# Whole or tiled turns on TensorE in an attention-then-mixing kernel, with a new order of its steps

## The chip, the cores and the metric

The kernel runs on one core of one Trainium2 chip. The metric is the device time of one execution in microseconds; the median of three timed runs of the kernel before is 230.54 us. Engines are named as in the profile: PE (TensorE, matmuls), PEld (its weight loads), DVE (VectorE), ACT (ScalarE), POOL (GpSimd) and SP (SyncE, which only issues DMAs here; a few of the last stores are issued by ACT).

## The reference: what is computed

For 8 batches, 8 heads, 576 positions and 64 features per head, attention is computed twice: once on q, k and v averaged over groups of four positions (144 of them) and repeated fourfold, and once locally, each position looking at those less than four away. The two are added and taken as x, 576 x 512 per batch. Then x is mixed:

```python
theta = x @ w_theta
zr, zi = x * np.cos(theta), x * np.sin(theta)
y = np.einsum('ts,bsd->btd', w_tok_r, zr) + np.einsum('ts,bsd->btd', w_tok_i, zi)
u = x + y
return (u + np.maximum(u @ w_ch, 0.0)).astype(np.float32)
```

Inputs and the output are float32; inside, the kernel works in bfloat16 with float32 sums.

## The kernel before, in words

The work of all eight batches is cut into named steps, and one string, `ORDER`, lists them: some 1190 words. A word's first two letters name the kind of step, the rest its place: the banks of PSUM on which a PE step works (`tp67`: banks 6 and 7), the engine of a copy (`a` ACT, `v` DVE, `g` POOL) or the staging slot of a load (base 36). Each kind is handed its batches and parts in ascending order, so the string alone fixes the order. After each word the function `pin` ties every instruction to the one before it on its engine; each engine, and SP's queue of DMAs, thus runs exactly in the order of the string, each at its own pace, and semaphores hold it where data or buffers are not ready. Three batches or so are under way at a time.

Per batch the steps are:

- `lk`, `lq`, `lv`, `lw`: loads of k, q (four of 288 KB each) and v into 16 staging slots, issued on SP. `ck`, `cq`, `cv`: their casts to bfloat16. Line 295 casts q and k, line 396 v.
- `tp` (function `tp`, line 302): turns a pair of head pairs of k or q, [positions, features], to [features, positions]. A partition holds nine positions, so that nine blocks are turned into two PSUM banks. `ev` (line 315) copies the result out to `kT` and `qT`. For batch 7 the DMA turns them (`dk`).
- `kd`, `qd`: sums over four positions (lines 321, 329 to 335). `pv`, `vd`: the same for v.
- `sd`, `ed`, `nd`, `xn`, `xd`, `xc`: the averaged attention, up to its turned result `xdT`.
- `ps` (line 482), `ex`, `mk`: local scores, exponential and band, in blocks of 64 positions; `po` (line 515) and `nm` (lines 523 and 524): times v, and the division, into `tmp`.
- `xt` (line 537): turns the local result by matmuls against an identity, in units of two, two and one chunks per batch (a chunk is 116 positions). `xa` (line 545) adds the averaged result and writes `xT`.
- `th`, `cs`, `tt`, `ct`: theta and its cosine and sine (line 556 on PE, 561 and 562 on ACT). `xm`, `zz`, `zt`, `zp`, `zc`: x turned and multiplied by them, into `z`. Batches 6 and 7 turn x by DMA (`dx`).
- `mx` (line 636) and `ua` (line 641): the mix over tokens, eight groups of nine matmuls, and the addition of x.
- `up`, `uc` or the DMA `du`: u turned back. `ch` (line 666), `rl` (line 674) and `st`: the channel product, the rectified sum and the store; `ht`, `rt`, `ss`, `sr` do this for the last 64 positions, two batches at a time.

Once, at the start, the weights are loaded and cast (`la`, `ca`, `lb`, `cb`, `lc`, `cc`), the token weights are turned on PE (`wp`, `wc`), and v of batch 0 goes its own way (`l1`, `c1`, `t1`, `e1`, `x1`). `wm` words (line 764) are matmuls on zeros: the bank, a number of 512-column ones and one of so many times 64 columns. `te` and `ts` touch the exponential or the sine on ACT.

Each PE step uses the array in one of these shapes: whole (128x128) for `tp`, `xm`, `up`, `th`, `tt`, `mx`, `ch`, `ht`, `wp`, `nd` and `xd`; 64x64 tiles for `ps`, `po`, `sd` and `xt`; 128 rows by 32 or 64 columns for `pv` and `x1`. In a row of the profile the shape stands ahead of the operands, as in `64*64 64x58`.

Of the kernel before, what the change touches and what calls it, by code (L numbers as in the profile page):

```python
# [63 lines left out]
wcv xm2 cbg xm0 zz zp7 tp45 cs qdg wp3 wp6 zz wcv lw zz wcv wcv zca eva wp7 wcv wp1 wca te wp0 wcv ps34 ps56 ex ex
ps12 mx0 lq1 cvg lk2 lka mx7 lqc mx3 qdv cvg ua lk7 ex ua lk0 mkv mkv kdg sd67 po45 nm sd12 lq4 cva lk5 lk9 cvg cvg ed
ed mx0 ua ua lq3 pv67 po45 po23 nm mx0 vda mkg nd67 lk8 nd45 lkb nm xn xn lq6 ckg ckg tp12 mx3 po45 ua lca ua nm cqg
cqg tp67 eva eva xd0 ckg ckg up1 lq7 po23 lvc xcv nm tp45 xt67 cqg mx0 cqg xt23 eva xt45 lv4 qdg kdg uca lw lv0 lw lw
lv3 lv1 lw lw xa xa tp67 cka ts ckg ckg th1 th2 xa th5 lk8 xm4 evv cs cqg xm1 ckv th3 zz tt4 up6 lq6 lqb cs zz tp12
xm7 ua cs ucv ct cs cqg eva te ztv xm6 zz zz mx0 ua tp34 zp7 tp56 ps12 zcv mx7 mx0 ex cvv kdg evv eva lk7 lk9 cvg lk4
qdg ua up7 uca sd12 mkv ps34 po56 ex ua ccv lcc lc5 kdg nm mkv mx0 sd34 ed po56 cvg cvg ua cqg mx7 nm ua ed mx0 ua lk2  # L70
cka cqg ps67 lqd lq0 cva po45 nm lca ex po23 ckg ckg nm pv01 lvb mx6 vda lk6 utv lw tp45 eva lv1 lw cca ccv nd01 nd23
ua xn xn qdg tp67 mx5 eva lv8 lv9 cqg cqg lw lw ccg ps34 qdg ps67 ua ps12 kdv ex ex xd0 lva xca lw mkg mkg lqc lq0 ch5
rl ckg ckg cvg cvg ch3 sd67 xt45 mkg ed rl ex ts mx0 xa xt67 po45 lv5 th1 cs xa nm ua tp23 th7 up4 up1 ucv xt56 xa mkv
lv4 ch0 eva po56 po23 cvg lq2 tt4 uca th1 cs th7 nm st nm xm2 lqb rl lq1 zz lqd ct cvg xm6 lw cqg ch5 cs zz cs cqa te
up0 up1 rl sd23 ucv po67 ch4 nm rl ch0 rl ucv tp67 lv7 ed cvg pv45 vdv lk8 lk9 eva st st tp23 eva xm0 ztg lk0 lka lw
xm1 zz zz zp7 ch6 zca lvc lv3 kdg nd45 xn nd23 ckg tp01 cva xn qdg utg mx7 cka ps23 rl kdg eva ps01 ua po45 mx6 up7 ex
ex lw lw lv8 nm qdg lw cqg po45 cqg ucv lvb lv2 lw sd23 sd01 lv5 ed mx7 lw lw ua tp23 nm xd4 ed ckg ckg xca st evv
tp01 eva mx6 mkg xt45 xt23 ua ua cva cvg cvg xt01 cka ts cvg xa xa mx7 th6 xa po45 nm pv23 tt0 th1 lk4 xm4 st st mkg
th5 vdv st cs nd23 ua zz ct cqg cqg ztg tp67 th4 cs dt po01 cs cs te xn evv po23 mx5 kdg qdg xm4 xm6 mx7 nm ps01 ex nm
ps23 ua lvd ua ex ch5 ps01 ex qdg zz lw lw xm7 zz rl kdg zp6 zz mkg nd23 xn lv1 lva lv3 mx5 zca sd67 lw ps01 ex po34  # L80
mx2 ua lw ed tp01 sd67 cva nm po34 eva cvv cvg ed lw up5 uca ua mx2 cvg nm cvg lvc xd3 ua pv04 xcv lk7 lk0 mx7 lq9 lq6
lq2 lqd lq8 lqb lq5 ckg ckg vda lq7 lw xt56 mkv cqg cqg po34 lk4 xt01 xa xa ch2 st cva ts lv6 th5 up6 ckg xm0 nm th1
tp34 cs ucv cs mkg rl eva mx6 ua ua th1 xt67 lk0 lk1 cs cqa po45 mkv xa nm ht3 rt tp67 th1 eva zz xm2 lv9 xm3 xm4 lw
lve zz zz ckg dk4 kdv mx0 cqg tp67 nd23 xn cs zz ua cqa eva mx1 nd67 xn cqa sr cqa cka tt2 ct dkb up4 cva cva ua mx0
mx7 ua cvg cvv uca te po01 nm qdg kdg qdg sd56 ed po23 ua ch4 rl xd0 ch1 ztg lw nm up7 ch4 uca xca po23 dz xt67 rl evg
ckg nm st st pv15 vda mx0 ps23 xa ex rl up1 up7 evg ua ucv mx6 uca ss ps01 ex xt45 cqa utg xa ua lv1 dk4 ps23 ex mx7
up0 uca th4 lvb sd56 mkv po23 lw lw xt01 utg dt ua dk7 cvv nm th7 du ed ts evg nd56 xa nd23 tt0 xn xn ct qdg mkv mkg
evv mx1 ztg xd2 up0 ua cs ch3 rl cs te mx4 ch7 qdg ps56 rl xcv ua mx1 ex cvg po23 po45 ua uca ps67 ex ht1 nm nm st st
rt cva ss mx0 ua po67 xt45 nm ps23 st xa ex ts du kdg th1 xm0 xm7 cs th6 cs xm4 zz zz zz ch5 rl kdg mx7 ua th0 po67 nm
cs te xt45 xa sd12 ch3 xm0 ch7 ch4 xt56 st ed sd12 mkg mkg ed ts zz dz lw mx0 lv1 du du cvv lw cvg th1 cs rl uta mx3  # L90
st rl rl xa dxb ua po45 po67 pv02 nm nm ua du mx1 vda ch4 dx mkg ua po23 po01 po67 rl sr nm mx5 ua mx4 tt5 dx1 du nm
nm nd23 xn nd01 st mx6 th7 mx2 cs xn xd3 mx0 ua ua xcv ua ua xt67 utv ct dx st st xt45 xt23 xa ch1 rl th0 ch6 ch1 ch7
cs xa xa tt0 zz zz th2 th3 cs st du du ch4 rl zz zz ztg ct dz rl mx2 mx0 mx1 cs ua ua st dxe dx ht0 ua th1 cs th3 dx7
dx zz st st mx2 rl mx1 ua ua cs zz dt mx3 mx1 mx2 zz zz ztg dz mx7 ua mx3 du du du mx6 rt ua ua utg ua st rl du st mx7
mx4 ua ua ua sr mx7 mx6 mx5 ua ua ua du du ua ch7 ch6 ss ch5 rl rl ch7 ch6 ch4 ch3 du du st uta dt sta rl st rl ht7
ch2 sta rl st rl sta rl st rt ssa sr rl sta rm su k0
"""


# [1 line left out]
def kernel(  # L101
# [161 lines left out]
    at = {}  # L263
# [32 lines left out]
        return step  # L296

    def tp(b, i, n, w):
        ps = at["tp", b, i, n] = pair(w).rearrange("p k e -> p (k e)").bitcast(BF16)
        t = tm[n][(2 * b + i) % TM]  # L300
        for r in range(WR):
            nc.tensor.transpose(out=ps[:, P * r:P * r + P], in_=t[:, r, :, :], identity=ident)  # L302
# [15 lines left out]
    def means(src, dst, w):
        with nc.allow_low_precision(reason="sums are taken in float32 and rounded once"):
# [205 lines left out]
                                in0=ps[:, :, :, 0:D], in1=r.unsqueeze(3).to_broadcast([P, 2, 4, D]), op=ALU.mult)  # L525

    def xt(b, u, w):
        ps = at["xt", b, u] = pair(w).rearrange("p k (x n) -> p (k x) n", x=2)
        for i, c in enumerate(UNITS[u]):
            t = tmp[(NCH * b + c) % NTMP]  # L530
            for g in range(2):
                n = 2 * c + g
                lo = STEP * n - W0[n]
                for j in range(4):
                    for hf in range(2):
                        r = slice(W * hf, W * hf + W)
                        nc.tensor.matmul(out=ps[W * (j % 2):W * (j % 2) + W, 2 * hf + j // 2,  # L537
                                                CH * i + STEP * g:CH * i + STEP * g + OWN[n]],
                                         lhsT=t[r, g, D * j:D * j + D], rhs=ident[r, W * hf + lo:W * hf + lo + OWN[n]],
                                         start=True, stop=True)  # L540
# [267 lines left out]
```

## Time and profile before

| | |
|---|---|
| timed runs | 230.54, 230.37, 230.74 us |
| span of the profiled execution | 232.2 us |
| share of the span in which the engine is busy | PE 94%, DVE 81%, ACT 67%, POOL 62% |
| costliest lines on PE | L636 (`mx`) 78.0 us, L556 (`th`) 30.8, L666 (`ch`) 29.8 |
| lines of the change on PE | L302 (`tp`) 252 matmuls, 19.2 us; L537 (`xt`) 640 matmuls, about 10 us |
| moved by DMA | 49.41 MB, 213 GB/s in the mean |

The profile gives the profiled execution's span, from the first instruction to the last; no other time was kept of that execution. A row of a group reads: line, engine, operation, output and inputs, shape, count, then busy time and the mean duration of one, then the idle time ahead of it and what ended it. The busy time of PE counts an instruction until its result has gone through the array, so neighbours overlap: the time that a group takes from PE is read from the start of its first instruction to the start of the next group's first.

### The profile page before, as it was taken

The page shows a single profiled execution, that of the slowest core. Times are in us where ns is not written, and L with a number is a line of the kernel's source. Part 1 is how long each engine was busy: PE and PEld are TensorE (multiplying, and loading weights), DVE is VectorE, ACT ScalarE, POOL GpSimd, SP SyncE. Part 2 cuts the span into 40 slices and gives each one's busy share as a digit, 9 for nine tenths or more (in the row PEclk, how much of TensorE's full clock was granted, in tenths as well). Part 3 has the DMA queues.
Part 4 walks back from the last instruction along what each step waited for, and adds up shares of the span by engine and source line. Part 5 has one row for each costly group of instructions (what it writes and reads, how often), then busy time and mean ns, then how long its engine had stood idle before and what let it go on. Part 6 is the DMA issues. An engine that isn't in the chain of part 4 may idle for free.

```text
span 232.2 us, 9404 instructions
## 1 busy us (share of the span) xinstructions
PE 217.7 (94%) x3943; PEld 152.6 (66%) x3970; DVE 187.7 (81%) x367; ACT 156.2 (67%) x243; POOL 145.0 (62%) x192
## 2 busy tenths in 40 slices
PE   7997899999999999899999989989998999999992
PEld 3655678877877666776775675756655775668741
DVE  5699888999988799789968887698986978558473
ACT  4589799689988898898877978778788232430000
POOL 7689977879985999879963489598952001100000
PEclk9999799999999999999999999999999999999999
DMA  6999968997999689968999996892284358656587
GB/s 217 395 390 390 291 114 238 361 300 118 265 391 179 165 245 285 243 142 214 205 165 347 307 213 115 206 153 92 67 149 109 71 127 193 138 159 137 142 227 245
DMA packets 76795, 49.41 MB, mean 213 GB/s; under 512 B 61136, under 2 KB 61392, under 8 KB 76752
## 3 DMA queue, kind: packets, MB, share of 16 engines
q1 hardware_dynamic: 76096, 47.76, 81.9%
q10 hardware_dynamic: 656, 1.05, 1.3%
q8 instruction: 31, 0.51, 0.9%
q14 instruction: 12, 0.10, 0.1%
HBM read 33.98 MB, written 9.44 MB: 187 GB/s over the span
## 4 chain that ended last, share of the span: by engine, by line
PE 60%; DMA 10%; POOL 10%; issue 6%; ACT 5%; DVE 4%; SPq 4%; DVEq 0%; POOLq 0%; ACTq 0%
PE PS L636 21%; PE PS L666 9%; PE PS L556 8%; DMA st<-in_q_dram 6%; PE PS L302 4%; POOL two L329 3%; PE PS L515 2%; SPq L347 2%; DMA st<-in_k_dram 2%; PE PS L537 2%; DMA ur<-uT 2%; POOL q_tm L295 2%; PE PS L482 2%; PE PS L447 1%; PE PS L595 1%
## 5 line engine op out<-in xcount | busy, mean ns | idle before, releaser
L636 PE MATMUL PS<-WT,z 128*128 128x288 bf16 x576 | 78.0, 287 | 0.0
L636 PEld LDWEIGHTS <-z 128*128 128x128 bf16 x576 | 53.9, 98 | 15.9 <-issue 1.3
L641 DVE TENSOR_TENSOR uT<-PS,xT 128x288 bf16<-128x288 f32 x64 | 28.6, 452 | 12.7 <-PE PS L636 10.9
L561 ACT ACTIVATE cs<-PS,pihc 128x512 bf16<-128x512 f32 x32 | 22.0, 689 | 21.1 <-PE PS L556 13.4
L556 PE MATMUL PS<-wth,xT 128*128 128x512 bf16 x116 | 30.8, 383 | 0.7 <-issue 0.2
L666 PE MATMUL PS<-wch,uT 128*128 128x512 bf16 (+1 forms) x122 | 29.8, 373 | 0.9 <-issue 0.6
L524 DVE TENSOR_TENSOR tmp<-PS,rl 128x512 bf16<-128x512 f32 x40 | 27.7, 692 | 1.4
L545 DVE TENSOR_TENSOR xT<-PS,xdT 128x928 bf16<-128x928 f32 (+1 forms) x24 | 22.3, 952 | 3.7 <-PE PS L537 2.3
L674 DVE SCALAR_TENSOR_TENSOR osb<-PS,ur 128x512 f32<-128x512 f32 x28 | 19.1, 687 | 7.1 <-DMA ur<-uT 3.0
L490 ACT ACTIVATE pm<-PS 128x1024 bf16<-128x1024 f32 (+1 forms) x24 | 20.5, 880 | 6.2 <-PE PS L482 6.1
L577 POOL TENSOR_TENSOR zT<-xT,cst 128x512 bf16<-128x512 bf16 x7 | 9.7, 1383 | 20.6 <-ACT cst L574 20.6
L295 POOL CAST k_tm<-st 128x576 bf16<-128x576 f32 x23 | 15.1, 668 | 11.2 <-DMA st<-in_k_dram 11.1
L396 POOL CAST v_w<-st 128x512 bf16<-128x512 f32 x21 | 13.3, 651 | 10.6 <-DMA st<-in_v_dram 10.5
L770 ACT ACT_TABLE_LOAD x15 | 19.2, 1283 | 0.3
L666 PEld LDWEIGHTS <-uT 128*128 128x128 bf16 x132 | 11.9, 98 | 11.2
L562 ACT ACTIVATE cs<-PS 128x512 bf16<-128x512 f32 x32 | 19.1, 597 | 0.0
L556 PEld LDWEIGHTS <-xT 128*128 128x128 bf16 x128 | 11.7, 99 | 10.6 <-issue 0.6
L295 POOL CAST q_tm<-st 128x576 bf16<-128x576 f32 x23 | 15.4, 686 | 4.9 <-DMA st<-in_q_dram 4.7
L503 POOL TENSOR_TENSOR pm<-pm,band 128x512 bf16<-128x512 bf16 x16 | 18.3, 1164 | 0.0
L329 POOL TENSOR_TENSOR two<-qT 128x576 f32<-128x576 bf16 x14 | 16.5, 1177 | 0.7 <-ACT qT L315 0.4
L620 DVE TENSOR_TENSOR z<-PS,cs 128x1024 bf16<-128x1024 bf16 x24 | 15.8, 684 | 0.5 <-ACT cs L562 0.3
L437 ACT ACTIVATE pd<-PS 128x864 bf16<-128x864 f32 x16 | 13.8, 889 | 2.5 <-PE PS L426 2.5
(124 smaller groups left out, 422.9 us busy)
## 6 DMA issues: line engine op xcount, KB each, us to landing
st<-in_k_dram SPq DMA_DIRECT2D x32, 288.0 KB, 6.5
st<-in_q_dram SPq DMA_DIRECT2D x32, 288.0 KB, 6.3
st<-in_v_dram SPq DMA_DIRECT2D x70, 128.0 KB, 5.2
out_dram<-osb SPq DMA_DIRECT2D x26, 256.0 KB, 4.0
st<-in_v_dram SPq DMA_DIRECT2D x4, 288.0 KB, 3.5
st<-in_moe_w_tok_r_dram SPq DMA_DIRECT2D x4, 288.0 KB, 6.5
st<-in_moe_w_tok_i_dram SPq DMA_DIRECT2D x4, 288.0 KB, 7.2
st<-in_moe_w_theta_dram SPq DMA_DIRECT2D x4, 256.0 KB, 6.7
```

Of the source, the lines that this page charges most:

```text
L295: COPY[w](out=to, in_=of)
L329: nc.gpsimd.tensor_tensor(out=t, in0=src[:, :, 0:2], in1=src[:, :, 2:4], op=ALU.add)
L490: nc.scalar.activation(out=pm[(3 * b + u) % NPM][:, :, 0:n].rearrange("p e c j w -> p e (c j w)"), in_=at.pop(("ps", b, u))[:, :, 0:4 * W ...
L524: nc.vector.tensor_tensor(out=tmp[(NCH * b + c) % NTMP].rearrange("p g (j d) -> p g j d", d=D), in0=ps[:, :, :, 0:D], in1=r.unsqueeze(3).t ...
L545: nc.vector.tensor_tensor(out=xT[b % 2][:, :, lo:lo + cnt].rearrange("p e (m j) -> p e m j", j=4), in0=at.pop(("xt", b, u))[:, :, 0:cnt].r ...
L556: nc.tensor.matmul(out=ps, lhsT=xT[b % 2][:, dc, P * c:P * c + P], rhs=wth[:, dc, :], start=(dc == 0), stop=(dc == 3))
L561: nc.scalar.activation(out=t[:, 0, :], in_=ps, func=AF.Sin, bias=pihc, scale=1.0)
L562: nc.scalar.activation(out=t[:, 1, :], in_=ps, func=AF.Sin, bias=0.0, scale=1.0)
L636: nc.tensor.matmul(out=ps, lhsT=z[b % 2][:, j, P * dc:P * dc + P], rhs=WT[:, j, cols], start=(j == 0), stop=(j == 8))
L641: nc.vector.tensor_tensor(out=uT[b % 2][:, dc, cols], in0=at.pop(("mx", b, i)), in1=xT[b % 2][:, dc, cols], op=ALU.add)
L666: nc.tensor.matmul(out=ps[:, cols], lhsT=uT[b % 2][:, dc, P * c:P * c + P], rhs=wch[:, dc, cols], start=(dc == 0), stop=(dc == 3))
L770: nc.scalar.activation(out=idle, in_=pihc, func=TABLE[kind])
```

## The change

`tp` gets a second form, chosen by a `q` behind the banks: 36 transposes in 64x64 tiles (nine blocks, two halves of the input partitions, two of the output partitions), with each half of the input in a bank of its own. `xt` keeps its tiled form behind a `q`; without it, a chunk is turned by four matmuls over the whole array. `ev` and `xa` read PSUM accordingly.

The order string is written anew. The kinds and numbers of the steps stay the same, but for the fillers. What differs, by count:

| words | before | after |
|---|---|---|
| `tp` whole / tiled | 28 / 0 | 4 / 24 |
| `xt` whole / tiled | 0 / 24 | 6 / 18 |
| `wm` | 6 words, 27 x 512 columns and 5 shorter | 4 words, 15 x 512 and 3 shorter |
| `ck` + `cq` on ACT / DVE / POOL | 16 / 2 / 46 | 16 / 13 / 35 |
| `ev` on ACT / DVE / POOL | 20 / 9 / 3 | 22 / 8 / 2 |
| `cv` on ACT / DVE / POOL | 13 / 6 / 21 | 12 / 4 / 24 |
| `kd` + `qd` on DVE / POOL | 5 / 27 | 3 / 29 |
| `uc` on ACT / DVE | 9 / 7 | 6 / 10 |

Staging slots, PSUM banks and the places of the loads on SP's queue differ throughout.

```diff
 ORDER = """
-kcg l10 l11 l12 l13 kcv lk4 lq5 c1a wm7e0 kcg c1g t101 lk6 lk7 ckg c1a ckg c1v t123 e1a kcv e1v wm737 tp01 x12 cqa x13
-lq8 x14 cka x15 cqg evv cva lk9 tp67 ckg cvv cva lqa lqb tp01 lk1 cqg x14 cva wm521 evv evv cqa qdv tp23 cva la3 eva
-pv47 vda wm624 ps01 kdg la6 ps23 ex kdv ckg lq4 ex wm656 wm717 lq2 ps01 qdg lk5 sd67 mkv ckv cqg sd45 po23 ed lk8 cag
-ed ex po67 lq9 lba nm cba nd45 nm nd23 xn cag mkg cqa tp01 po67 xn po45 nm lkb eva xd0 mkg ckg lq7 cka xca la1 po23 nm
-tp67 cag xt45 la0 xt01 nm lb3 lb4 lb5 cqg lbc xa lba lb2 xt23 xa eva tp67 lb8 cqg lb1 caa ts th4 kdg cs cbg xm5 xa lv7
-evv lw th0 th2 lv0 cbv lw zz cbg tt3 xm4 lv3 cs cbg cbv ct cbg cbg cs lvb lw lw wp0 wcv wp1 wcv ztg wp5 th3 wp1 lv8
...
+l10 l11 l12 l13 lk4 lk5 c1a te lq6 lq7 lk0 c1g c1g c1a wm090 t101 cqg kcg lk8 lq9 ckv e1a cqg t123 cka ckg e1v kcv
+wm443 tp01 x12 lqa lq1 lk3 lb4 lk5 lb6 la7 lk0 x13 x14 ckg kcg cvv cvv lb8 cqg tp56q x17 lb9 lk2 lqb eva tp23 x10 cva
+eva cqg cvv kdv eva wm112 tp45q cva kdv kcv eva cka pv23 vdv wm113 ps01 qdg qdg ex ps45 ex mkv lba ckv la3 lac lad cbg
+lq5 lq4 lbe ps67 sd23 cbg ed lb6 lbf sd01 po45 cbg cqg po23 lb1 ed mkv nm tp01q nm nd45 lv8 xn nd23 ex eva cqa po01 xn
+nm mkg cag cbg kdg cba cag cag po67 tp45q eva wp2 xd3 xca cag wca xt01 cqg ckg wp4 cbg qdg cbg cbg nm xa xt56 wp7 wp2
+po01 xa th3 wcv lva lw nm cka wcv cbg lw lve ts cs cqa lk1 th5 xm4 xm6 xt01 xa zz cs th7 cs zz tp01q lvf lw tt3 evv
+wcv ct ztg lw lv6 lw xm5 th4 cs tp67q wp0 zz eva wp1 xm2 wp3 zp5 wp4 ps67 wcv wcv zz wca ps01 kdg wcv wp2 ps34 zcv wcv
+mx5 qdv cvg mx2 ex mkv ex sd67 ua ex lk8 lq4 cva lqa ed po01 mkv mx5 nm cvg ckg lqe ua lk1 po34 lk0 sd01 cva cvg ed
+po67 nm ua mx2 po34 pv05 nm ckg cqg xt67q mkg cqg mx1 ua nm vda ckg cqg ckg ts nd45 nd23 ua xn mx1 tp45 xn ua xd2 eva
+lqf xcv xa lq6 lk5 mx1 tp23q xt45q lvd lk8 lv4 xa po67 nm eva th0 cs xm2 cqv lqa lkc th5 lve lkf xt67q lw tp34q th0 xa
+lk0 lw lq1 lv2 lw cs cs lw lv3 ua zz evv tt1 tp67 eva xm2 th5 xm0 lw zz ct zz up4 xm2 ps67 cs mx3 ztv ucv zp4 zz zcv
+mx0 qdg cqg ckg kdg ckg ckg cqg kdg ua ckv cvg tp23q qdg ex tp45q tp67q ua eva up1 eva mx0 mkv ps23 po45 evv ua nm
+sd67 mx0 ed ckv ua ex ucv mx6 up7 uca cvg kdg cqg ps01 ua mkv cvg sd23 cvg lcd po45 ex cva lq4 lcf nm up6 lca lk0 lvc
+mx7 pv45 ccv ua ed vda mkg qdg po01 ccg po23 kdg ccg lv1 lce lw lqd lq3 lw mx7 nm lvf cqa lq4 lv2 lw lka lk8 cka nd45
+lk0 lq5 lv6 lw nm ucv ua tp01q nd23 lw mx7 xn xn lk9 ccg eva tp01q ps45 xd6 ch2 ua ex xca evv xt34q xt01q cva ps56 mx7
+ex cva cqa qdg rl xa ch4 xa ua po56 nm sd01 ps23 th7 ed ex mkg cqv ckg xt56 up0 ch1 th2 xa ucv rl tt0 tp34q po56 cs rl
...
+xt01q xt67q mx2 xa mx3 ch4 ch5 xa ch0 xa ua du st dx0 dx utg tt2 rl ua mx1 ch3 th4 rl ua mx1 th5 dx1 du cs dx th4 cs
+ct ua cs st mx1 sr ztg ua th5 du rl du mx2 st zz dt ch4 mx0 mx1 ua rl zz ua zz ht0 cs rl zz ch4 st dz du mx5 ua du st
+mx1 ua mx5 mx3 mx2 rl rt mx0 mx4 uta ua mx1 ua ua ua ua ch0 ch5 ch2 ch3 ua ch4 sr st ss st du ua ch1 ch6 du du du rl
+st rl rl rl utg sta te ch5 ht0 k0 rl rl rl rm rl dt st te sta st sta st su rt sta sr ssa te
 """
...
@@ -296,10 +296,20 @@
         return step
 
     def tp(b, i, n, w):
-        ps = at["tp", b, i, n] = pair(w).rearrange("p k e -> p (k e)").bitcast(BF16)
         t = tm[n][(2 * b + i) % TM]
-        for r in range(WR):
-            nc.tensor.transpose(out=ps[:, P * r:P * r + P], in_=t[:, r, :, :], identity=ident)
+        if w[2:] == "q":
+            ps = pair(w[:2]).bitcast(BF16)[:, :, 0:W * WR].rearrange("p a (r w) -> p r a w", w=W)
+            for r in range(WR):
+                for a in range(2):
+                    for x in range(2):
+                        nc.tensor.transpose(out=ps[W * x:W * x + W, r, a, :], in_=t[W * a:W * a + W, r, x, :],
+                                            identity=ident[W * a:W * a + W, W * a:W * a + W])
+        else:
+            ps = pair(w).rearrange("p k e -> p (k e)").bitcast(BF16)[:, 0:P * WR]
+            for r in range(WR):
+                nc.tensor.transpose(out=ps[:, P * r:P * r + P], in_=t[:, r, :, :], identity=ident)
+            ps = ps.rearrange("p (r a w) -> p r a w", a=2, w=W)
+        at["tp", b, i, n] = ps
 
     def dk(b, i, n, w):
         to = at["dk", b, i, n] = stg[int(w, 36)].bitcast(BF16)
@@ -313,7 +323,7 @@
                     in_=at.pop(("dk", b, i, n)).rearrange("p (r a w) -> p a w r", a=2, w=W))
             return
         COPY[w](out=to[:, 2 * i:2 * i + 2, 0:S].rearrange("p a (w r) -> p a w r", r=WR),
-                in_=at.pop(("tp", b, i, n))[:, 0:P * WR].rearrange("p (r a w) -> p a w r", a=2, w=W))
+                in_=at.pop(("tp", b, i, n)).rearrange("p r a w -> p a w r"))
 
     def means(src, dst, w):
         with nc.allow_low_precision(reason="sums are taken in float32 and rounded once"):
@@ -525,27 +535,35 @@
                                 in0=ps[:, :, :, 0:D], in1=r.unsqueeze(3).to_broadcast([P, 2, 4, D]), op=ALU.mult)
 
     def xt(b, u, w):
-        ps = at["xt", b, u] = pair(w).rearrange("p k (x n) -> p (k x) n", x=2)
+        ps = pair(w[:2]).rearrange("p k (x n) -> p k x n", x=2)
+        quad = w[2:] == "q"
         for i, c in enumerate(UNITS[u]):
             t = tmp[(NCH * b + c) % NTMP]
             for g in range(2):
                 n = 2 * c + g
                 lo = STEP * n - W0[n]
-                for j in range(4):
-                    for hf in range(2):
-                        r = slice(W * hf, W * hf + W)
-                        nc.tensor.matmul(out=ps[W * (j % 2):W * (j % 2) + W, 2 * hf + j // 2,
-                                                CH * i + STEP * g:CH * i + STEP * g + OWN[n]],
-                                         lhsT=t[r, g, D * j:D * j + D], rhs=ident[r, W * hf + lo:W * hf + lo + OWN[n]],
-                                         start=True, stop=True)
+                cols = slice(CH * i + STEP * g, CH * i + STEP * g + OWN[n])
+                if quad:
+                    for j in range(4):
+                        for hf in range(2):
+                            r = slice(W * hf, W * hf + W)
+                            nc.tensor.matmul(out=ps[W * (j % 2):W * (j % 2) + W, hf, j // 2, cols],
+                                             lhsT=t[r, g, D * j:D * j + D], rhs=ident[r, W * hf + lo:W * hf + lo + OWN[n]],
+                                             start=True, stop=True)
+                    continue
+                for k in range(2):
+                    nc.tensor.matmul(out=ps[:, k, :, cols], lhsT=t[:, g, P * k:P * k + P],
+                                     rhs=identw[:, :, lo:lo + OWN[n]], start=True, stop=True)
+        at["xt", b, u] = ps if quad else ps.rearrange("p k x n -> p x k n")
 
     def xa(b, u, w):
         lo = 2 * CH * u
         cnt = min(2 * CH, S - lo)
         nc.vector.tensor_tensor(
-            out=xT[b % 2][:, :, lo:lo + cnt].rearrange("p e (m j) -> p e m j", j=4),
-            in0=at.pop(("xt", b, u))[:, :, 0:cnt].rearrange("p e (m j) -> p e m j", j=4),
-            in1=xdT[b % 2][:, :, lo // 4:(lo + cnt) // 4].unsqueeze(3).to_broadcast([P, 4, cnt // 4, 4]),
+            out=xT[b % 2][:, :, lo:lo + cnt].rearrange("p (x k) (m j) -> p x k m j", k=2, j=4),
+            in0=at.pop(("xt", b, u))[:, :, :, 0:cnt].rearrange("p x k (m j) -> p x k m j", j=4),
+            in1=xdT[b % 2][:, :, lo // 4:(lo + cnt) // 4].rearrange("p (x k) m -> p x k m", k=2).unsqueeze(4)
+            .to_broadcast([P, 2, 2, cnt // 4, 4]),
             op=ALU.add)
```

More of the change, by code (lines that the diff above doesn't have):

```diff
@@ L63 @@
-evv lw th0 th2 lv0 cbv lw zz cbg tt3 xm4 lv3 cs cbg cbv ct cbg cbg cs lvb lw lw wp0 wcv wp1 wcv ztg wp5 th3 wp1 lv8
[L64 to L96, printed above, removed]
+l10 l11 l12 l13 lk4 lk5 c1a te lq6 lq7 lk0 c1g c1g c1a wm090 t101 cqg kcg lk8 lq9 ckv e1a cqg t123 cka ckg e1v kcv
@@ new lines @@
+mkv cs evv th7 ct cqg ckg cs th2 ztg cvg cqg cvg nm po34 tp01q up5 xm7 cvg ch6 cs eva kdg nm ckv qdg ckg uca te xm2 st
+ch3 rl lv8 lq4 zz lw st lv0 lv6 lq2 lk5 lvf sd01 ed lqa lw po45 zz kdg rl pv67 lw ch2 lw lv9 lq3 xm3 nm rl zz tp01q
+vda ch4 xm7 nd23 up6 zp5 zz eva nd01 uca tp67q zca xn ps23 qdg mx5 rl utv xn ex eva po01 ps23 mx4 sd67 ex lkd lw st
+lk1 lvc st lqe lw lv7 mkv ua nm lw sd23 ua cqv po01 nm ed mx5 xd4 xt67 cka kdg cvg mx0 mx1 ua cqv xca ed ts cva cqv
+xt23q xa tp67q mkg mkg ua ckg cvg eva cvg xa cvg xt45q th0 up2 th3 tp67q cs cs ua cqv xa tp01q ucv po45 ch2 xm3 evv
@@ new lines @@
+pv67 eva po01 nm rl vda th4 tt2 th7 nd56 ct cs cs zz mx2 ps34 nm xn po56 ps01 mx7 ua xm2 nm ua nd56 ex cka ex qdg lv9
+lvf lv6 ztg utg lk3 lw lkd lq0 lqa dt lq2 lw lw lv1 lk5 lw zz lv8 zp7 xm4 xm3 xn zz zca mx2 qdg kdg mkg ua zz sd67
+ps45 po01 mx2 ed nm ex cqa xd7 po01 sd34 ps56 ua mx2 nm up0 cvg te ex xcv ckv ed ua up7 xt34q cqg mkg cvg uca cva
+tp56q xa xt12q ht0 mx3 xa cvg rt cvg xt12q eva ucv po45 nm xa ua pv06 mx7 tp12q vda ts ua evv po45 ch3 nd67 nm xn th0
+nd45 kdg th1 cvg ckg cqa cqg cka mkg mkg cs qdg xn tp67q tp45q cs mx0 tt1 evv xd2 xm6 xm7 st lw st lq7 lv3 lk6 lk9 lvf
@@ new lines @@
+lqe ua rl th0 xcv zz lw st lv2 lk5 sr lw eva ct ts up2 mx1 xm6 kdg th3 qdg utg ztg lw ts cqg ckg lva st lqd lq1 dz mx4
+cs zz ckv zz cs ucv ts cvg po56 ua cvv nm po01 sd23 ch7 mx5 nm ps01 rl ua ua ed ps67 po23 xm4 ch5 ex ex up0 up1 utv nm
+cvg ckg cqg uca zz mx2 uca mkv xt34q sd01 st lw lkf ua dk8 rl po67 mkg nm xa ch2 mx5 dke ss evg ed cqa cva ps67 xt01q
+cka ua pv34 xa ex vdv xm5 th6 xt01 th7 xa up3 mx4 cqa rl cs dkf st dk1 lv8 ch2 lw lv2 st ua lw dt st lvd nd01 mx4 tt6
+xn rl ucv up0 cs evg up1 th7 qdg mkg eva nd23 ct ch6 eva cs cva ucv zz ucv ua xn qdg kdg ps45 po23 ps01 rl nm mx7 xd6
@@ new lines @@
+mx2 ex ex th5 po01 ps34 ua mkv xcv ua nm kdg ztg cvg po67 mx2 mkg cs ex xm0 ch1 nm ch5 ua xm2 xm6 mx7 rl zz zz zz ht2
+xt34q ua rl po67 sd01 lw du du st dz lv8 rt xa st lw st ss du du mx5 mx2 ed te ts xt34q sd01 ua nm cva xa ua ed xt67q
+mx5 th4 cs po23 xa ua nm cvg cvg mkg po67 pv01 mx5 ch2 nm rl mx4 ua uta po23 vda po56 po01 ua nm tt7 nm mx4 th2 nd56
+nm xn dx1 dx nd01 mx3 ch5 ct cs ua ztg du dx2 dx st dz zz xn du st th4 cs th0 xd1 mx2 rl zz ua xcv cs zz ua zz xt45q
+xt01q xt67q mx2 xa mx3 ch4 ch5 xa ch0 xa ua du st dx0 dx utg tt2 rl ua mx1 ch3 th4 rl ua mx1 th5 dx1 du cs dx th4 cs
```

## The prediction

> **What bounds the kernel now.** I read the page first: span, busy times, granted clock.
>
> ```profile
> span 232.2 us, 9404 instructions
> ...
> PE 217.7 (94%) x3943; PEld 152.6 (66%) x3970; DVE 187.7 (81%) x367; ACT 156.2 (67%) x243; POOL 145.0 (62%) x192
> ...
> PEclk9999799999999999999999999999999999999999
> ```
>
> The profiled span is 232.2 us and the median of the timed runs 230.54, so profiling lengthens the execution by 1.7 us; I take differences from the profile and subtract them from 230.54. PE is the fullest engine, but 94% is an average. So next came busy time by stretches (columns: stretch, its length, then busy us and instruction counts of PE, PEld, DVE, ACT and POOL, the granted clock, DMA share, GB/s).
>
> ```profile
> 0.00:20.00 20.00, 17.05 (x272) 9.88 (x275) 15.40 (x39) 13.47 (x20) 15.66 (x39) 1.00 0.93 342
> 20.00:40.00 20.00, 18.36 (x402) 14.91 (x404) 17.57 (x35) 17.85 (x28) 17.17 (x23) 0.91 0.87 238
> 40.00:60.00 20.00, 19.95 (x426) 15.30 (x425) 18.67 (x37) 16.41 (x26) 16.93 (x23) 1.00 0.93 256
> ...
> 100.00:120.00 20.00, 19.70 (x453) 14.21 (x453) 18.63 (x35) 16.56 (x26) 18.18 (x23) 1.00 1.07 191
> 120.00:140.00 20.00, 18.51 (x297) 13.29 (x299) 15.71 (x28) 16.61 (x28) 10.49 (x15) 1.00 1.17 269
> ...
> 180.00:200.00 20.00, 19.74 (x323) 13.05 (x326) 16.80 (x35) 5.97 (x14) 1.16 (x1) 1.00 0.60 138
> ...
> 220.00:232.00 12.00, 7.86 (x41) 3.79 (x39) 6.75 (x11) 0.40 (x1) 0.00 (x0) 1.00 0.76 230
> ```
>
> From 40 us on PE is without work for 0.05 to 1.5 us in 20; only the first 40 us and the last 4 have larger holes. DVE comes second, over 18.6 of 20 in two stretches. So PE work taken away after 40 us moves the end by nearly its length, provided that DVE follows. The question is therefore what a turn costs PE, from the start of its first matmul to the start of the next group (a row's own duration contains the pipeline's latency). The timeline of PE shows this.
>
> ```profile
> 99.81 0.42 PE L466 MATMUL PS<-ident,xdn 72*128 72x72 bf16 x8
> 100.07 0.67 PE L302 MATMUL PS<-ident,k_tm 128*128 128x128 bf16 x9
> 100.57 1.27 PE L636 MATMUL PS<-WT,z 128*128 128x288 bf16 x9
> 101.77 0.86 PE L537 MATMUL PS<-ident,tmp 64*64 64x58 bf16 x80
> 102.56 1.28 PE L636 MATMUL PS<-WT,z 128*128 128x288 bf16 x9
> ```
> ```profile
> 109.73 0.45 PE L515 MATMUL PS<-v_w,pm 64*64 64x65 bf16 x32
> 110.11 1.28 PE L636 MATMUL PS<-WT,z 128*128 128x288 bf16 x9
> 111.22 0.61 PE L595 MATMUL PS<-ident,xT 128*128 128x128 bf16 x8
> ```
>
> Start to start, a whole turn of q or k (L302, nine instructions) takes 100.57 - 100.07 = 0.50 us, 55.6 ns each. In 64x64 tiles 80 instructions take 102.56 - 101.77 = 0.79 and 32 take 110.11 - 109.73 = 0.38: the 48 between them cost 0.41, so **8.5 ns each**, four tiles running side by side, and 0.38 - 32 x 0.0085 = **0.11 us** is what it takes to leave the tiles. Entering them shows in L636: nine take 111.22 - 110.11 = 1.11 ahead of a whole group, and 101.77 - 100.57 = 1.20 ahead of tiles: **0.09 us**.
>
> **The change part by part.**
>
> *Turns of q and k (`tp`).* 24 of 28 go from 9 whole transposes to 36 in tiles. No transpose in 64x64 tiles runs before, so the price is bounded: below by 8.5 ns (L537 is the same turn against the same identity, as a matmul with a float32 result), above by a transpose that shares the array with nothing, L466: eight in 100.07 - 99.81 = 0.26, or 32 ns. I take 8.5, since L537 agrees in tiles, operand and width. That is 36 x 0.0085 = 0.31 against 0.50: -0.19 each, **-4.6 us** for 24. The upper end would be 36 x 0.032 = 1.15 each, +0.65, +15.6 in all. The copies that follow (`ev`) read as many elements, in as many instructions; nothing is added there.
>
> *Turns of the local result (`xt`).* 6 of 24, with 9 of the 40 chunks, go the other way. A chunk had 16 tile matmuls, 16 x 8.5 = 0.136 us, and gets 4 whole ones of 116 columns. From 128 columns (55.6 ns) and 288 (1.11 / 9 = 123 ns) a column is worth 0.42 ns, so 116 take 50.6 ns and a chunk 0.20: +0.07, **+0.6 us** for nine. The addition after it (`xa`) reads the same elements in another order; I take it as equal.
>
> *Changes of tile shape.* Read along the two order strings, neighbouring steps on PE differ in tile shape 107 times before and 115 times after; at 0.09 to 0.11 that is **+0.8 us**. That a tiled turn alone among whole steps saves nothing follows too: 0.31 + 0.09 + 0.11 = 0.51 against 0.50.
>
> *PE's sum:* -4.6 + 0.6 + 0.8 = **-3.2 us**.
>
> *The start.* The filler matmuls (`wm`, L764) shrink from 27 of 512 columns and five shorter to 15 and three.
>
> ```profile
> L764 PE MATMUL PS<-warm 128*128 128x512 bf16 x25 | 6.7, 395 | 0.2 <-issue 0.2
> ...
> L295 POOL CAST k_tm<-st 128x576 bf16<-128x576 f32 x23 | 15.1, 668 | 11.2 <-DMA st<-in_k_dram 11.1
> ...
> L295 DVE CAST k_tm<-st 128x576 bf16<-128x576 f32 x2 | 1.5, 742 | 0.0
> ```
>
> They fill time in which PE waits for loads, casts and copies, so I count their absence at nothing. If nothing had been late, it would be worth 12 x 0.216 = 2.6 us (the time of a 512-column matmul by 0.42 ns a column). The other piece of the start is the granted clock, 0.91 over 20 to 40 us: the equivalent of 0.09 x 20 = 1.8 us of PE. One such dip may vanish or come twice; I take it as unchanged. The set of steps that stands ahead of the first token mix (`mx` of batch 0, whose row on PE follows) is the same in both orders. The loads of the token weights (`lb`) stand earlier. Start: 0, between -4.4 and +1.8.
>
> ```profile
> 36.89 3.36 PE L636 MATMUL PS<-WT,z 128*128 128x288 bf16 x26
> ```
>
> *Other engines.* Casts of q and k go from POOL (46 to 35) to DVE (2 to 13): 11 x 0.742 = +8.2 us on DVE, of which about 6 are taken off again (`ev`, `kd`, `qd`, `cv`, `c1`, `cb`, `wc` and `cc` each lose one or two there, `uc` gains three, `xc` and `zc` one). Net, DVE gets some 2 us, out of 232 - 188 = 44 of idle time; its cover is PE's queue, and where that is gone is the second rival below.
>
> *DMA and queues.* The loads, DMA transposes and stores are as many as before, in another order on SP, with other slots. What matters is how long ahead of its cast a load is issued.
>
> ```profile
> st<-in_k_dram SPq DMA_DIRECT2D x32, 288.0 KB, 6.5
> st<-in_q_dram SPq DMA_DIRECT2D x32, 288.0 KB, 6.3
> ```
>
> The median landing takes 6.3 to 6.5 us. In PE work that stands between the two words, the first q load of batch 2 led its cast by some 8.4 us and now by 3.3; k and q of batch 6 and v of batch 7, which had leads down to nothing, get 5 us or more. POOL's 11.1 us of waiting for k loads is the price that short leads have now. I take the sum over the batches as zero, with -2 to +3.
>
> *The tail.* After the last mix both orders leave PE eight channel groups and one last one, and DVE the same ten additions; only the last piece is another one. 0, give or take 0.3.
>
> **Sum:** 230.5 - 3.2 = **227.3 us**.
>
> **The rivals.**
>
> 1. *The gain is larger because the start shortens too.* For it: fewer fillers, earlier weight loads, 1.8 us of lost clock to win back. Against it: PE's holes in the first 40 us come from loads and copies that are not fewer. Taking the fillers whole: 227.3 - 2.6 = 224.7.
>
> 2. *Another engine or a load becomes the bound, and most of the gain is given back.* Between the last mixes of batches 1 and 2, six more casts of q and k land on DVE (+4.4 us, +2.4 after what it loses there); PE's own sum is 0.7 less there.
>
> ```profile
> 70.00:99.00 29.00, 27.94 (x614) 19.72 (x616) 24.95 (x49) 25.27 (x36) 25.62 (x33) 1.00 0.95 221
> ```
>
> This is about that stage: DVE at 24.95 of 29 us would stand at 27.3, level with PE, and a DVE that is late delays every mix, whose banks it empties. With the short leads of batch 2 (6.3 - 3.3 = 3 us late at worst) the loss is 2 to 4 us: 227.3 + 3 = 230.3, no change. Against it: batches overlap, so neither engine waits for the other at one place only.
>
> 3. *Slower: tiled transposes do not run side by side.* Place: the 24 turns. Point: a turn in tiles breaks even, with the 1.4 us of the other two terms spread over 24, at (0.50 - 0.06) / 36 = 12.3 ns per instruction; every ns above it costs 0.9 us. At L466's 32 ns the end is 230.5 + 15.6 + 1.4 = 247.5. For it: no such transpose is in this trace, and L466 and L302 cost what their columns cost. Against it: L537 at 8.5 ns.
>
> [...]
>
> 4. *The change does not do what it says to the neighbours:* tiles are meant to match their neighbours, yet the count of shape changes rises. This is in the sum already; were a change three times its 0.1 us, the extra 1.6 us would give 228.9, still faster.
>
> **How the numbers follow.** The forecast (225.8 to 228.8, its own range, with rival 4 at its edge): 0.52. Rival 1 (224 to 225.8): 0.14. Rival 2 (228.8 to 231.5): 0.23, of which 0.08 still faster, 0.08 within 0.2%, 0.07 slower. Rival 3: 0.07. Other ways to lose (a load or a store far behind on SP's queue): 0.04. A measurement of this kernel tells 0.2%, some 0.46 us, from no change. So faster 0.74, same 0.08, slower 0.18. The range goes from rival 1 with half of the lost clock won back, 227.3 - 2.6 - 0.9 = 223.8, to rival 2 with its whole 4 us, 231.3; rival 3 stays outside it.
>
> **What would show it.** Right: the turns of q and k as 64*64 groups of 36 at about 0.31 us start to start inside a tiled block; PE's busy time down by some 3 us beside the fillers' share; PE still without holes from 40 us on. Wrong: 36 instructions at 0.45 us or more; DVE over 19 of 20 us with PE waiting for it between 60 and 100 us; POOL waits for batch 2's loads that PE then shares; a first mix that starts clearly before or after 36.9 us; a second dip in the granted clock.

## The result, and the profile after

The changed kernel takes 243.98 us in the median (242.18 to 246.44, four runs) against 230.64 for the kernel before: 1.055 times as long, with a 95% interval of 1.049 to 1.061. The ratios and intervals in this text compare fast runs with fast ones alone (the profiled execution, 246.44 us, counts as slow), so they are not quite the quotients of the medians beside them. The forecast was 227.3, range 223.8 to 231.3. Neither the sign nor the size was right.

The page of the changed kernel:

```profile
span 244.7 us, 10444 instructions
...
PE 218.0 (89%) x4465; PEld 151.9 (62%) x4496; DVE 188.4 (77%) x368; ACT 160.5 (66%) x241; POOL 141.9 (58%) x192
...
PEclk9995899997999859999999999999999999999999
...
q8 instruction: 35, 0.57, 1.0%
```

PE is busy as long as before (218.0 us) in a span that is 12.5 us longer; no other engine has become full. What is new is idle PE, and three stretches of low clock where there was one. By stretches (columns as in the prediction):

```profile
0.00:20.00 20.00, 14.83 (x313) 8.75 (x315) 14.97 (x40) 13.67 (x17) 15.12 (x38) 0.99 0.94 339
20.00:40.00 20.00, 17.03 (x434) 13.78 (x436) 16.54 (x31) 17.05 (x27) 17.23 (x24) 0.84 0.90 230
40.00:60.00 20.00, 17.02 (x388) 12.18 (x389) 15.52 (x30) 11.68 (x18) 12.66 (x18) 0.93 0.89 241
...
80.00:100.00 20.00, 16.27 (x372) 9.80 (x364) 13.58 (x22) 13.23 (x21) 9.93 (x15) 0.83 0.80 182
100.00:120.00 20.00, 19.05 (x525) 13.81 (x527) 17.80 (x34) 17.58 (x26) 18.76 (x23) 1.00 0.99 217
...
180.00:200.00 20.00, 19.79 (x356) 13.84 (x359) 17.38 (x36) 13.88 (x22) 7.50 (x9) 1.00 0.57 120
```

From 40 to 60 us PE was busy for 19.95 us before and is for 17.02 now; from 80 to 100 us for 16.27 against 19.19, as this row of the kernel before shows:

```profile
80.00:100.00 20.00, 19.19 (x380) 13.71 (x381) 17.08 (x36) 17.25 (x25) 18.77 (x25) 1.00 0.94 243
```

DVE, my rival, falls with it. From 180 to 200 us PE is as full as before (19.79 us against 19.74). What PE waits for stands in its waits (who waited for whom: us in total, times, longest), here of the changed kernel:

```profile
PE PS L492 <- issue: 5.9, 4, 3.3
PE PS L305 <- issue: 3.1, 2, 2.5
PE PS L457 <- issue: 1.9, 1, 1.9
...
PE PS L525 <- issue: 1.2, 1, 1.2
...
PE PS L574 <- issue: 0.5, 3, 0.2
```

and of the kernel before:

```profile
PE PS L515 <- issue: 0.7, 1, 0.7
PE PS L666 <- issue: 0.6, 4, 0.2
...
PE PS L650 <- issue: 0.5, 1, 0.5
```

"issue" means that the profile shows nothing that PE waited for: no semaphore, no buffer, no other engine. These waits make 12.6 us in the rows shown now, against 1.8 in those of before (what is left out are waits of 0.2 each, three in either kernel). And they stand in odd places, as the timeline of the changed kernel's PE shows:

```profile
79.61 0.48 PE L305 MATMUL PS<-ident,k_tm 64*64 64x64 bf16 x36
79.92 0.44 PE L492 MATMUL PS<-qT,kT 64*64 64x64 bf16 x32
...
81.52 0.75 PE L550 MATMUL PS<-ident,tmp 64*64 64x58 bf16 x64
82.09 0.34 PE L492 MATMUL PS<-qT,kT 64*64 64x64 bf16 x16
85.72 0.43 PE L492 MATMUL PS<-qT,kT 64*64 64x64 bf16 x16 [3.30 <-issue]
86.08 2.34 PE L654 MATMUL PS<-WT,z 128*128 128x288 bf16 x9
```

One step `ps` of 32 matmuls, whose operands all lie ready, stops in its middle for 3.3 us. The first row also settles what the prediction turned on: a tiled turn takes 79.92 - 79.61 = 0.31 us, as forecast. After the wait L654 takes 2.34 us for nine, where it took 1.27: the granted clock has fallen to 0.50. Two stretches of the same kernel show the wait and the clock behind it:

```profile
82.30:85.70 3.40, 0.12 (x15) 0.01 (x2) 2.08 (x3) 0.27 (x1) 2.38 (x3) 0.81 1.13 267
84.40:91.20 6.80, 5.26 (x73) 3.10 (x75) 1.00 (x3) 2.39 (x4) 2.17 (x4) 0.50 1.16 258
```

**The reading that the experiments test (theory I).** The page counts what queue q8 ("instruction") moved: 35 packets, 0.57 MB, thus 16 KB each. Before it was

```profile
q8 instruction: 31, 0.51, 0.9%
```

PE and its weight loads have 4465 + 4496 = 8961 instructions now and 3943 + 3970 = 7913 before: some 256 for each packet in both kernels. So q8 brings PE's instructions, in blocks of 256. The packet that belongs to the wait above lies in it; the DMA queues between 82.6 and 84.1 us show

```profile
q8 instruction: 1, 0.02, 6.1%
```

and none in the 0.4 us before or the 1.6 us after. Counting two instructions for each of PE's weight loads (some records of matmuls are missing), all the waits over 1 us for "issue" begin within 6 instructions of the end of such a block (the ends fall 64 short of the multiples of 256, as if some instructions had run before the program's own). So does one of 1.2 us in the middle of an `xt` at 136.5 us, which the profile puts down to DVE. PE goes on 1.3 to 1.7 us after the packet's end. From the start of a block to that of the next, 3.8 to 6.4 us pass in these places. By the rates that the prediction read from the kernel before (8.5 and 123 ns), a block of 128 loads and 128 matmuls lasts, as an estimate, 128 x 8.5 ns = 1.1 us in 64x64 tiles and 128 x 123 ns = 16 us as whole matmuls of 288 columns. A tiled turn is 72 instructions where a whole one was 18; 24 of them add 1296, most of them beside other tiled steps: 18 of the 24 have one as a neighbour on PE.

Theory O is the rival that stood in the prediction in parts: the new order itself is slow, by late loads, a thinner start, fewer fillers. Theory T: turns in tiles are slow in themselves.

### The profile page after: what moved, and what is told of

It reads as the page before. It is cut to its first block, busy times and chain, and to the rows that moved or that the text cites. A ratio compares the mean times of both kernels' runs of the same rounds, so it can differ in the third digit from the quotient of the medians.

```text
span 244.7 us, 10444 instructions
## 1 busy us (share of the span) xinstructions
PE 218.0 (89%) x4465; PEld 151.9 (62%) x4496; DVE 188.4 (77%) x368; ACT 160.5 (66%) x241; POOL 141.9 (58%) x192
## 4 chain that ended last, share of the span: by engine, by line
PE 72%; issue 9%; DVE 8%; ACT 5%; DMA 2%; POOL 1%; SPq 1%; ACTq 0%; DVEq 0%
PE PS L654 28%; PE PS L684 10%; PE PS L574 10%; PE PS L305 3%; PE PS L525 2%; PE PS L492 2%; PE PS L550 2%; DMA st<-in_q_dram 2%; PE PS L457 2%; PE PS L613 2%; PE PS L462 2%; PE PS L718 1%; PE PS L586 1%; PE PS L436 1%; PE PS L668 1%
## 5 line engine op out<-in xcount | busy, mean ns | idle before, releaser
L654 PE MATMUL PS<-WT,z 128*128 128x288 bf16 x576 | 80.2, 289 | 0.5 <-ACT cs L580 0.3
L654 PEld LDWEIGHTS <-z 128*128 128x128 bf16 x576 | 54.2, 98 | 16.6 <-issue 1.1
L574 PE MATMUL PS<-wth,xT 128*128 128x512 bf16 x113 | 31.6, 387 | 1.3 <-issue 0.5
L684 PE MATMUL PS<-wch,uT 128*128 128x512 bf16 (+1 forms) x119 | 30.6, 378 | 1.0 <-issue 0.4
L595 POOL TENSOR_TENSOR zT<-xT,cst 128x512 bf16<-128x512 bf16 x7 | 8.1, 1154 | 33.5 <-ACT cst L592 33.5
L339 POOL TENSOR_TENSOR two<-qT 128x576 f32<-128x576 bf16 x15 | 17.4, 1161 | 6.6 <-ACT qT L325 3.6
L339 POOL TENSOR_TENSOR two<-kT 128x580 f32<-128x580 bf16 x14 | 16.6, 1184 | 7.5 <-ACT kT L325 4.0
L574 PEld LDWEIGHTS <-xT 128*128 128x128 bf16 x128 | 11.5, 99 | 13.3 <-issue 3.9
L684 PEld LDWEIGHTS <-uT 128*128 128x128 bf16 x132 | 12.4, 99 | 11.6 <-issue 1.1
L513 POOL TENSOR_TENSOR pm<-pm,band 128x512 bf16<-128x512 bf16 x14 | 16.3, 1191 | 1.8 <-ACT pm L500 1.8
L406 POOL CAST v_w<-st 128x512 bf16<-128x512 f32 x24 | 14.6, 626 | 3.3 <-DMA st<-in_v_dram 3.3
L492 PE MATMUL PS<-qT,kT 64*64 64x64 bf16 x640 | 10.4, 198 | 6.2 <-issue 5.9
```

The source lines that it names most:

```text
L339: nc.gpsimd.tensor_tensor(out=t, in0=src[:, :, 0:2], in1=src[:, :, 2:4], op=ALU.add)
L513: EW[w].tensor_tensor(out=t[:, x], in0=t[:, x], in1=m[:, x], op=ALU.mult)
L574: nc.tensor.matmul(out=ps, lhsT=xT[b % 2][:, dc, P * c:P * c + P], rhs=wth[:, dc, :], start=(dc == 0), stop=(dc == 3))
L654: nc.tensor.matmul(out=ps, lhsT=z[b % 2][:, j, P * dc:P * dc + P], rhs=WT[:, j, cols], start=(j == 0), stop=(j == 8))
L684: nc.tensor.matmul(out=ps[:, cols], lhsT=uT[b % 2][:, dc, P * c:P * c + P], rhs=wch[:, dc, cols], start=(dc == 0), stop=(dc == 3))
```

## The experiments

**1. The new order without tiled turns of q and k.** Every `q` behind a `tp` word is taken off, nothing else:

```diff
-... tp01 x12 ... tp56q x17 ... tp45q ... tp01q ...
+... tp01 x12 ... tp56 x17 ... tp45 ... tp01 ...
```

> The new order, slots, engines and fillers, with all 28 turns of q and k whole and the turns of the local result as in the changed kernel: 1296 instructions of PE fewer than the changed kernel. Theory I (instruction supply: PE is fed its instructions in blocks of 256, and a block that is used up in under about 4 to 6 us makes PE wait for the next): the waits go, 229 to 233 us, PE's own sum being 0.5 us above the kernel before. Theory O (the new order itself is slow: late loads, fewer fillers, clock dips): 240 us or more.

Measured: 233.2 us (231.67 to 234.41), 1.014 times the kernel before (1.006 to 1.022). So the 24 tiled turns cost 10.8 us of the 13.3, in an order that was made for them, where PE's own sum says that they save 3.7 (from +0.5 to -3.2). Of PE's waits in this kernel none over 0.2 us is for "issue"; the longest are

```profile
PE PS L226 <- DVE warm L197: 1.3, 1, 1.3
PE PS L436 <- DVE vd L425: 0.5, 1, 0.5
```

Theory I holds for the bulk. The remaining 2.5 us, 0.5 of which are PE's sum, are the order's.

**2. The old order with tiled turns of q and k.** The same 24 of 28 turns, by number, get their `q`; all `xt` keep tiles:

```diff
-... tp01 x12 cqa x13 ... tp67 ckg cvv ... xt45 ...
+... tp01 x12 cqa x13 ... tp67q ckg cvv ... xt45q ...
```

> The order of the kernel before, with the same 24 of 28 turns of q and k in tiles and all turns of the local result in tiles: 1296 instructions of PE more than the kernel before, 28 more changes of tile shape, PE's own sum 2.6 us less. Theory I: PE waits for blocks of instructions, 238 to 246 us. Theory O: nothing of the new order is in it, so it follows PE's sum, 228 to 230 us.

Measured: 242.58 us (240.66 to 244.2), 1.053 (1.044 to 1.062). Nothing of the new order is in it, and it loses 11.8 us where PE's sum is a gain of about 2.0 (24 turns at 0.19, less 26 more changes of shape at 0.1; the 2.6 of the expectation doesn't come out of these rates): 13.8 us to explain, much as in experiment 1 (10.8 + 3.7 = 14.5). The waits for "issue" are there,

```profile
PE PS L550 <- issue: 3.8, 2, 2.4
PE PS L492 <- issue: 3.5, 4, 1.9
```

and the page has one packet for each 256 instructions again (4618 + 4618):

```profile
PE 223.3 (92%) x4618; PEld 150.9 (62%) x4618; DVE 187.5 (77%) x367; ACT 156.8 (65%) x243; POOL 145.7 (60%) x192
...
q8 instruction: 36, 0.59, 1.1%
```

**3. Fewer instructions elsewhere.** The changed kernel with every `xt` whole, `tp` as it is:

```diff
-... xt67q mkg cqg ... xt45q lvd ...
+... xt67 mkg cqg ... xt45 lvd ...
```

> The changed kernel with all turns of the local result whole (18 of 24 were tiled), the turns of q and k left in tiles: 744 instructions of PE fewer, PE's own sum 2.1 us more. Theory I: about half of the waits go, 236 to 240 us. Theory O: 244 us or more, by PE's sum.

Measured: 237.79 us (236.56 to 240.56), 1.030 (1.021 to 1.039). 744 instructions fewer and 2.1 us more of PE's work make the kernel 6.2 us faster, and its waits for "issue" fall from 12.6 to 4.0 us. Of the theories, only I says so.

**4. The cost by itself.** A kernel that computes nothing of the reference, and only feeds PE:

```python
whole(60); tiles(1536, 64); whole(60); tiles(768, 256); whole(60)   # (matmuls, columns)
for _ in range(1536):
    nc.tensor.matmul(out=PS[:, 4, 0:64], lhsT=warm[:, 0:128], rhs=warm[:, 0:64], start=True, stop=True)
```

> Measures the disputed cost by itself: a kernel that leaves out all of the computation and loads nothing. PE alone gets 60 whole 512-column matmuls, 1536 matmuls of 64 columns in 64x64 tiles in a row, 60 whole, 768 of 256 columns in tiles, 60 whole, 1536 whole of 64 columns; zeros are stored at the end. Theory I: the 64-column tiles run at 8.5 ns for at most the 256 matmuls that are at hand, and then in bursts of 128 with waits between them, at a mean of 23 ns or more (128 in 3 us or longer); the 256-column ones, at some 27 ns each, wait little or not. If tiles are slow for another reason, the mean is above 8.5 ns without bursts; if instructions come as fast as PE takes them, it stays at 8.5 ns.

Measured once, in the timeline of its PE:

```profile
15.90 1.53 PE L30 MATMUL PS<-warm 64*64 64x64 bf16 x163
19.62 1.24 PE L30 MATMUL PS<-warm 64*64 64x64 bf16 x128 [2.19 <-issue]
...
30.80 1.92 PE L30 MATMUL PS<-warm 64*64 64x64 bf16 x128 [1.53 <-issue]
34.26 1.92 PE L30 MATMUL PS<-warm 64*64 64x64 bf16 x128 [1.53 <-issue]
37.71 1.92 PE L30 MATMUL PS<-warm 64*64 64x64 bf16 x128 [1.53 <-issue]
...
57.73 13.82 PE L25 MATMUL PS<-warm 128*128 128x512 bf16 x60
71.49 21.15 PE L30 MATMUL PS<-warm 64*64 64x256 bf16 x768
...
105.53 12.65 PE L39 MATMUL PS<-warm 128*128 128x64 bf16 x427
118.84 3.89 PE L39 MATMUL PS<-warm 128*128 128x64 bf16 x128 [0.66 <-issue]
123.11 3.89 PE L39 MATMUL PS<-warm 128*128 128x64 bf16 x128 [0.38 <-issue]
```

Bursts of exactly 128 matmuls, 256 instructions with their loads, come every 3.45 to 4.0 us, while the DMA engines move next to nothing else (2% busy). The mean is (57.73 - 15.90) / 1536 = 27 ns a matmul. In the same tiles 256 columns take 21.1 / 768 = 27.5 ns and never wait. Whole matmuls of 64 columns wait a little too, beside the stores of the zeros (128 in 4.3 us).

The first 163 matmuls, 326 instructions with their loads, ran without a wait; the 256 at hand of the expectation were the author's estimate and were not shown. Within a burst the tiled instructions took under 10 ns each (128 in 1.24 us at 19.62), or 15 at a granted clock of 0.50 (128 in 1.92 us at 30.80), and of the 27 ns in the mean some 12 are waits (1.53 us for 128 at 30.80). Whole matmuls of 64 columns took 30 ns each (427 in 12.65 us at 105.53).

**5. Instructions without turns.** The kernel before, with 16 matmuls of 2 columns added to each `po`, into columns that nobody reads:

```diff
                                      start=(j == 0), stop=(j == 3))
+        for _ in range(4):
+            for hf in range(2):
+                for g in range(2):
+                    nc.tensor.matmul(out=pair(w)[W * hf:W * hf + W, g, 400:402], lhsT=ident[W * g:W * g + W, 0:W],
+                                     rhs=ident[W * g:W * g + W, 0:2], start=True, stop=True)
```

> The kernel before, with whole turns of q and k, and 16 matmuls of 2 columns in 64x64 tiles added behind each of the 40 products with v, on zeros and ones of the identity, into columns that nobody reads: 1280 more instructions of PE, in the tiled stretches, and no tiled turn of q or k at all. At 8.5 ns they are 5.4 us of PE. Theory I (instruction supply): 5.4 us and again the 10 to 15 us of waits and lost clock that the tiled turns brought, 244 to 251 us. Theory T (the tiled turns are what is slow): 236 us, the added work alone.

Measured: 245.58 us (243.89 to 247.48), 1.064 (1.056 to 1.071). No turn was changed, and the kernel loses 15.1 us, 5.4 of which can be the added work. Theory T falls. The wait moves to whichever step stands at the end of the block, three times an unchanged `xt` (L555 in this kernel), here that of batch 0:

```profile
PE PS L555 <- issue: 6.2, 3, 2.3
```
```profile
26.34 0.57 PE L555 MATMUL PS<-ident,tmp 64*64 64x58 bf16 x25
28.98 0.95 PE L555 MATMUL PS<-ident,tmp 64*64 64x58 bf16 x55 [2.06 <-issue]
29.86 1.14 PE L310 MATMUL PS<-ident,k_tm 128*128 128x128 bf16 x9
```

**6. The fillers back.** The changed kernel with longer filler words:

```diff
-wm090 wm443 wm112 wm113
+wm0e0 wm474 wm1c2 wm153
```

> The changed kernel with its four filler words lengthened to 27 matmuls of 512 columns and some shorter ones, as many as the kernel before has. Theory I: the lost clock follows PE's waits for instructions and not the fillers, so nothing is won: 242 to 247 us. Theory O, in the form that too few fillers let the clock fall: 240 us or less.

Measured: 243.57 us (240.4 to 248.27), 1.050 (1.041 to 1.058): no clear difference from the changed kernel. The edit makes 14 + 7 + 12 + 5 = 38 fillers of 512 columns, more than the 27 of the expectation. The fillers are not what is missing.

**7. The old order with `xt` whole.** The old string in the changed program, where a plain `xt` is whole.

> The order of the kernel before with all turns of the local result whole: 960 instructions of PE fewer, PE's own sum 2.1 us more. Theory I: what the kernel before still loses at the ends of blocks (about 2 us) and some of its lost clock come back, 229 to 232.5 us; where instructions don't matter: 232.5 to 233 us, by PE's sum.

Measured: 231.47 us (230.57 to 232.63), 1.005 (1.002 to 1.008), inside the first expectation (PE's sum alone says 232.6). Of the 1.8 us of waits for "issue" in the kernel before, 0.3 are left, counted in the same way, so some of what it loses comes back, but less than the added work. The granted clock doesn't fall before the end (mean 0.993 in the profiled run); experiment 9 shows that this wins little.

**8. Only the turns that stand alone.** In the old order two `tp` between tiled neighbours go into tiles, two `xt` between whole neighbours go whole.

```diff
-... nm tp67 cag xt45 la0 ... nm tp45 xt67 cqg mx0 cqg xt23 ... xt56 ...
+... nm tp67q cag xt45q la0 ... nm tp45q xt67 cqg mx0 cqg xt23q ... xt56 ...
```

(The program is the changed one; the other `xt` of the old string get a `q` and so stay as they were.)

> The kernel before with only those turns changed that stand alone between neighbours of the other shape: two turns (k or q of batches 1 and 2) into tiles, two units of the local result (batches 1 and 2) whole. PE's own sum 1.0 us less, 8 changes of shape fewer, 36 instructions more. Theory I: so few instructions cost nothing, 229 to 230.5 us, up to 0.5% faster. Theory O or T: no difference, or slower.

Measured: 235.7 us (234.29 to 236.45), 1.023 (1.019 to 1.028). Theory I missed this one, and by its time alone the other expectation, "no difference, or slower", fits. But the trace shows the waits of theory I:

```profile
23.66 0.48 PE L305 MATMUL PS<-ident,q_tm 64*64 64x64 bf16 x36
24.50 1.15 PE L550 MATMUL PS<-ident,tmp 64*64 64x58 bf16 x78 [0.36 <-DVE tmp L534]
28.29 0.25 PE L550 MATMUL PS<-ident,tmp 64*64 64x54 bf16 x2 [2.64 <-issue]
```

The one tiled turn at 23.66 puts 54 more instructions ahead of 80 tiled matmuls, the block ends two matmuls before they are through, and PE waits 2.64 us; three such waits in `xt` make 4.2 us. It is not the number of instructions in the kernel that counts (36 more) but what stands in the 256 behind which the next block has to arrive.

**9. Fewer instructions where the kernel before is dense.** The old order, `xt` whole for batch 0, the first unit of batch 1 and the last of batch 2.

> The kernel before with the turns of the local result whole for batch 0, for the first unit of batch 1 and the last of batch 2, all else as before: PE's own sum unchanged to 0.1 us, 192 instructions of PE fewer, 120 of them in the dense stretch around 25 us where the kernel before waits at the end of a block and then loses clock. Theory I: that wait (0.9 us) and the lost clock (1.7 us) come back, in whole or in part: 228 to 230 us, up to 1% faster than before. If the place of the block ends matters less than that: 230 to 231 us, no difference.

Measured: 231.13 us (229.94 to 232.93), 1.003 (1.000 to 1.006): no difference. Its clock did not fall before the end (mean 0.997 against 0.993 in the profile of the kernel before), yet the time didn't follow. The record says why there was little to win: a stretch of 3.4 us at half speed brings the mean of this kernel down to 0.993, and of the 41 runs of the kernel before that are listed with these experiments 37 have 0.995 or more. The dip at 25 us in its profile is rare, and not part of its median. This version does not beat the kernel before, and none of the others does.

**10. The new order with all turns whole.** Experiments 1 and 3 together.

> The new order with all turns whole, of q and k and of the local result: 744 instructions of PE fewer than with the turns of q and k alone whole, PE's own sum 0.8 us more. If what that version still lost (1.4% against the kernel before) is instruction supply too: 231 to 232 us. If it is the order, the slots and the engines: 233.5 to 235 us.

Measured: 234.92 us (233.37 to 236.31), 1.019 (1.012 to 1.026): the second expectation. Fewer instructions bring nothing any more; the new order itself costs 2 to 3 us beyond PE's sum (2.5 - 0.5 in experiment 1, 4.4 - 1.3 here). Its first stretch,

```profile
0.00:20.00 20.00, 15.04 (x260) 8.73 (x261) 14.21 (x38) 13.48 (x17) 15.08 (x39) 1.00 0.92 335
```

has 2.0 us less of PE work than before in it (17.05). In experiment 1 it is 1.0 less (16.05), so a thinner start is likely; which load or slot makes it so was not tried.

## Why the prediction was wrong

*What bounds the kernel:* right in that PE was the bound and work on it the currency; wrong in "PE work taken away after 40 us moves the end by nearly its length". PE was also short of instructions here (12.6 us of waits for "issue" in the changed kernel), and the trace of before had the signs: 1.8 us of such waits, and a page line for q8 (31 packets). I read neither.

*Turns of q and k,* -4.6 us: the price of a turn was right (0.31 us). **The step that failed is the sum behind it:** it counts what an instruction takes of the array and nothing for its coming. By experiments 1 and 2 the same 24 turns cost +10.8 and +11.8 us. Of before's to after's 12.5 us, the rows give, as an estimate: waits for "issue" +10.8 (12.6 - 1.8), lost clock +6.2 (20 us times 0.16 + 0.07 + 0.17 = 8.0, against 1.8), PE's work -3.2; that makes 13.8, some of the lost clock falling on waits.

*Changes of tile shape* and *`xt`:* their sizes (0.1 us and 0.07 a chunk) were not contradicted. But an `xt` made whole is worth more than its row, where it takes 24 instructions a chunk out of a dense block (experiment 3: 6.2 us faster for 2.1 us more work).

*The start:* forecast 0. The first mix starts at 38.80 us, 1.9 later than before, and a thinner start remains with all turns whole. The fillers were rightly counted at nothing (experiment 6); the lost clock was not unchanged but came three times. Nor was there 1.8 us of it to win back, as rival 1 has it: the dip in the profile of before is one that most of its runs don't have (experiment 9).

*Other engines, DMA, tail:* as forecast. POOL's waits for k loads fell from 11.1 to 4.0 us, no stretch of DVE is fuller than 17.80 of 20, and PE ends 4.6 us before the span does, against 4.3.

*The rivals:* the third came nearest in time (247.5 us, at 32 ns an instruction, against 243.98), but that was luck: by its mechanism, turns that don't run side by side, it is refuted (0.31 us). The second (DVE or a load) didn't occur. None of the cases that shared the 0.18 for "slower" had the true mechanism in it.

*The base of the sum:* these runs list span and time of one execution together, 244.7 and 246.44, so some 1.7 us lie around a span. The execution profiled before (232.2) was then about 3.4 us slower than the median, and profiling doesn't lengthen it by 1.7; the terms of the sum, which are differences, are not touched. The 0.2% by which the prediction told a change from none was too fine: the 41 later runs of the kernel before lie between 228.69 and 233.44 us.

## What to carry to other kernels

Count PE's instructions, not only its time: for every run of 256 (a load and a matmul count two) add up their time from start to start, and where that falls under the time that a new block took here (3.45 to 6.4 us) look for a wait of PE. Waits that the profile puts down to "issue", in the middle of a step whose operands are ready, were the sign here (3.3 us in a `ps`). No run here was faster for splitting work into more and smaller tiles; the tiled instructions that never waited for the next block in experiment 4 were long ones (256 columns, 27.5 ns each).
